# Products over a head's 40 entries: whole stationary blocks of 128 columns, against halves of 64 that alternate between the four quarters of the array

## The chip, the cores and the metric

One core of one Trainium2 chip runs the whole program. The metric is device time in microseconds (us) of one execution of the program, from its first to its last work on the core; the time before is the median of two runs.

## The reference

The program computes two blocks one after the other, all in 32-bit floats. The first is a recurrence over 768 steps for 4 batch entries and 8 heads of 40 entries each; the second sends each of the 3072 result rows (8 heads x 40 = 320 wide) to one of 16 experts, each two matrix products with a relu between.

```python
for t in range(S):                       # S = 768, state is [B, H, D, D], D = 40
    y[:, :, t] = einsum('bhd,bhde->bhe', r_t, state)
    Sa = einsum('bhde,bhe->bhd', state, a_t)
    state = state * w_t[:, :, None, :] - einsum('bhd,bhe->bhde', Sa, b_t)
    state = state + einsum('bhd,bhe->bhde', v_t, k_t)
x = y.transpose(0, 2, 1, 3).reshape(B * S, H * D)
# gate: group by argmax of x @ w_group, expert in it by argmax of x @ w_expert[g]
ye = np.maximum(x @ w1[g, e], 0.0) @ w2[g, e]
out[token] = (weight of group) * (weight of expert) * ye
```

## The kernel before

**Part one** does the recurrence in chunks of 128 steps. There are 6 chunks for each of the 4 batch entries, 24 in all, and one loop (over `u`) goes through them, batch entry by batch entry within a chunk's place. In a chunk, all steps of a head are handled by matrix products of 128 x 128 blocks, one block per head.

A head's 40 entries lie on partitions, and two heads share a tile: the even head of a pair on partitions 0 to 39, the odd one on 64 to 103 (`blk(h)`; `HW` is 64, `NP` the 4 pairs). A chunk does, in the order of the text:

- four **products** over the 40 entries: `GT` from `Kt, At` (named in_k, in_a in the profile), `E` from `At, Bt` (in_a, in_b), `MT` from `Vt, Rt` (in_v, in_r), and near the chunk's end `NT` from `UT, Rt`. Each gives eight 128 x 128 blocks, one per head. `g` is 0 for the even and 1 for the odd heads; each `g` has its own PSUM tile `big` of 4 blocks, and VectorE copies it out through a mask that keeps one triangle (L228);
- VectorE sums the rows of `E` (L239) and makes a factor of them, GpSimd scales `E` by it (L244), TensorE transposes it (L247), ScalarE copies that out as `ET`;
- transposes of in_b, in_k and the running products pq (L217);
- the right-hand side `U` (L260 with the state `ST`, L263 with `GT`), and then seven levels (`lv`) that square `E` and `ET` (L273, L282) and apply `ET` to `U` (L293);
- `U` transposed (L304, `UT`), the next state (L314, L315), the product `NT`, the state transposed (L346), the chunk's result (L328, L332, L334), its transposes (L120) and the gate's logits (L131).

The Tile framework puts each engine's instructions in an order of its own choosing and sets the waits: the next chunk's first product stands around the gate's logits of the chunk before. Two pools of PSUM tiles set when a buffer comes free: five of `big` (512 columns each) and three of `small`. A 32-bit matmul stands in the profile as two loads of the stationary operand (PEld) and two passes of the moving one (PE); the transposes are one load and one pass.

**Part two** sorts the rows by expert and runs the experts by tiles of 128 rows (L558, L566). The change doesn't touch it.

Of the kernel before, what the change touches and what calls it, by code (L numbers as in the profile page):

```python
# [9 lines left out]
F32 = mybir.dt.float32  # L10
I32 = mybir.dt.int32
AX = mybir.AxisListType
ALU = mybir.AluOpType
# [4 lines left out]
# The chunked form of the recurrence divides by running products of w and inverts I + T by  # L18
# powers of T. Both are accurate while w stays within these bounds (128 factors make 1e-15 to
# 1e15) and no row of |T| sums to more than T_MAX. If an input breaks them anywhere, the  # L20
# recurrence is computed again a step at a time, in the reference's order.
# [4 lines left out]
def kernel(  # L26
# [15 lines left out]
    nc = tc.nc  # L42
# [29 lines left out]
    def big(shape):  # L72
        return psum.tile(shape, F32, tag="big", name="big", bufs=5)
# [9 lines left out]
    # up[s, t] = 1 for s < t; low[t, s] = 1 for s < t  # L83
# [10 lines left out]
    # A row of x_all is a token: its vector, its gate weight and its number.  # L94
# [10 lines left out]
    # Rows sorted by expert, each expert's share filled up to whole tiles. Rows that no token  # L105
    # takes keep a zero vector and a number beyond the last token.
# [9 lines left out]
    def transpose_x(pool, src):  # L116
        """[128 tokens, DM] -> [128, NK, 128 tokens]."""
        pt = big([P, NK, P])
        for ko, (k0, kn) in enumerate(KO):
            nc.tensor.transpose(pt[:kn, ko, :], src[:, k0:k0 + kn], ident)  # L120
        t = pool.tile([P, NK, P], F32, tag="xT", name="xT", bufs=2)
        nc.vector.tensor_copy(out=t[:, :NK - 1, :], in_=pt[:, :NK - 1, :])  # L122
        kn = KO[-1][1]
        nc.scalar.copy(out=t[:kn, NK - 1, :], in_=pt[:kn, NK - 1, :])  # L124
        return t
# [10 lines left out]
    # With P_t the product of w over the chunk's steps before t and Q_t that product through t,  # L136
    # A = a P, K = k / Q, B = b / Q and S the state at the chunk's start:
    #   (I + T) U = A S' + G V,         T[t, s] = B_s . A_t,  G[t, s] = K_s . A_t   (s < t)
    #   Y = P (R S + M K - N B),        M[t, s] = r_t . v_s,  N[t, s] = r_t . u_s   (s < t)
    #   next S = (S + V' K - U' B) Q_last  # L140
    # and (I + T)^-1 = (I - T)(I + T^2)(I + T^4)... exactly, T being strictly triangular.
    with ExitStack() as part:
# [18 lines left out]
        # The states of a pair of heads stand as the two diagonal blocks of a square that is zero  # L161
        # elsewhere: ST with the second axis of a state on the partitions, SN with the first.
# [14 lines left out]
        for u in range(NN):  # L177
# [4 lines left out]
            if u < NB:  # L182
                # the partitions that no head's rows take
                for nm in "wakbvr":
                    for q0 in (32, 96):
                        nc.any.memset(d[nm][q0:q0 + 32], 1.0 if nm == "w" else 0.0)
                nc.any.memset(d["pq"][:, :, 0:1], 1.0)
# [10 lines left out]
            # the running products of w (within its bounds), and a, k, b scaled by them  # L198
# [23 lines left out]
            def product(lhs, rhs, g, mask, name, bufs):  # L222
                ps = big([P, NP, P])
                for q in range(NP):
                    nc.tensor.matmul(ps[:, q, :], lhsT=lhs[blk(g), q, :], rhs=rhs[blk(g), q, :],  # L225
                                     start=True, stop=True)
                t = sb.tile([P, NP, P], F32, name=name, bufs=bufs)
                nc.vector.tensor_tensor(t, ps, mask, op=ALU.mult)  # L228
                return t

            # group 0 has the even heads, group 1 the odd ones
            GR = range(2)
            GT = [product(Kt, At, g, up4, "GT", 4) for g in GR]
            # T and its transpose; a row beyond its bound is scaled down to it
            E = [product(At, Bt, g, low4, "E", 6) for g in GR]
# [15 lines left out]
            MT = [product(Vt, Rt, g, up4, "MT", 4) for g in GR]  # L251
# [4 lines left out]
            # the right-hand side, then a factor of the inverse at a time  # L256
# [52 lines left out]
            # the next state  # L309
# [13 lines left out]
            # what the chunk returns  # L323
            NTm = [product(UT, Rt, g, up4, "NT", 4) for g in GR]
# [27 lines left out]
        # how often the bounds are broken  # L352
# [16 lines left out]
    with ExitStack() as part:  # L369
# [5 lines left out]
        # partition (q, b, h) holds rows q DQ .. (q + 1) DQ of the state of (b, h)  # L375
# [59 lines left out]
    with ExitStack() as part:  # L435
# [12 lines left out]
        def choose(vals, name):  # L448
            """The first largest of each token's values as a one-hot, and its softmax weight."""
# [34 lines left out]
        # each token's rank within its expert, then its row in xs  # L484
# [33 lines left out]
        # each tile's expert  # L518
# [81 lines left out]
```

## Time and profile before

| | |
|---|---|
| median of the runs | 2349.13 us (2348.99 to 2349.27) |
| the profiled execution, first to last instruction (span) | 2344.1 us |
| TensorE (PE) busy | 2137.4 us, 91% |
| stationary loads (PEld) busy | 1943.0 us, 83% |
| VectorE busy | 636.2 us, 27% |
| ScalarE busy | 416.2 us, 18% |
| GpSimd busy | 188.8 us, 8% |
| mean granted clock of TensorE | 0.806 of full |

The profiled execution's own time is its span, 2344.1 us; the median of the runs is 5.0 us more, which lies around the span. "Busy" of TensorE counts time in which any pass is under way, and passes overlap. The granted clock is 1.0 or 0.5 of full speed in a stretch (2.4 or 1.2 GHz); values between are means over stretches of both.

### The profile page before, as it was taken

The page shows a single profiled execution, that of the slowest core. Times are in us where ns is not written, and L with a number is a line of the kernel's source. Part 1 is how long each engine was busy: PE and PEld are TensorE (multiplying, and loading weights), DVE is VectorE, ACT ScalarE, POOL GpSimd, SP SyncE. Part 2 cuts the span into 40 slices and gives each one's busy share as a digit, 9 for nine tenths or more (in the row PEclk, how much of TensorE's full clock was granted, in tenths as well). Part 3 has the DMA queues.
Part 4 walks back from the last instruction along what each step waited for, and adds up shares of the span by engine and source line. Part 5 has one row for each costly group of instructions (what it writes and reads, how often), then busy time and mean ns, then how long its engine had stood idle before and what let it go on. Part 6 is the DMA issues. An engine that isn't in the chain of part 4 may idle for free. (4 is left out here: it accounts for less than half of the span.)

```text
span 2344.1 us, 32451 instructions
## 1 busy us (share of the span) xinstructions
PE 2137.4 (91%) x13731; PEld 1943.0 (83%) x13731; DVE 636.2 (27%) x1156; ACT 416.2 (18%) x766; POOL 188.8 (8%) x190
## 2 busy tenths in 40 slices
PE   4999999999999999999999999999505999999998
PEld 3999999999999999999999999999404677777676
DVE  6423333332333333233333232222300111111111
ACT  2222222121222212122212122222000000000000
POOL 3000000000000000000000000000021000000000
PEclk9878876687877868787767787777656999999999
DMA  6000000000000000000000000000042666666661
GB/s 186 21 12 18 21 17 19 20 18 12 18 18 18 21 21 18 12 18 18 18 21 18 12 13 18 4 1 1 29 155 88 212 212 215 200 202 217 205 212 51
DMA packets 143699, 152.68 MB, mean 65 GB/s; under 512 B 33529, under 2 KB 129534, under 8 KB 143552
## 3 DMA queue, kind: packets, MB, share of 16 engines
q1 hardware_dynamic: 133824, 136.21, 18.9%
q10 hardware_dynamic: 6704, 6.46, 1.0%
q0 software_dynamic: 3024, 7.90, 0.9%
q8 instruction: 111, 1.82, 0.3%
q14 instruction: 36, 0.29, 0.0%
HBM read 136.22 MB, written 16.78 MB: 65 GB/s over the span
## 5 line engine op out<-in xcount | busy, mean ns | idle before, releaser
L558 PE MATMUL big<-xT,w1s 128*128 128x128 f32 x1872 | 338.9, 312 | 25.3 <-DVE xT L122 24.6
L558 PEld LDWEIGHTS big<-xT,w1s 128*128 128x128 f32 x1872 | 259.3, 191 | 108.0 <-DVE xT L122 34.7
L293 PE MATMUL small<-U,ET 128*128 128x40 f32 x2688 | 345.9, 290 | 0.6 <-ACT ET L276 0.4
L293 PEld LDWEIGHTS small<-U,ET 128*128 128x128 f32 x2688 | 340.8, 205 | 2.3 <-ACT ET L276 0.5
L273 PE MATMUL big<-ET,E 128*128 128x128 f32 x2304 | 336.6, 292 | 0.0
L273 PEld LDWEIGHTS big<-ET,E 128*128 128x128 f32 x2304 | 300.7, 204 | 0.0
L282 PE MATMUL big<-E,ET 128*128 128x128 f32 x1920 | 266.0, 284 | 0.0
L276 ACT COPY ET<-big 128x512 f32<-128x512 f32 x288 | 168.8, 586 | 481.2 <-PE big L273 481.2
L282 PEld LDWEIGHTS big<-E,ET 128*128 128x128 f32 x1920 | 247.3, 201 | 0.0
L299 DVE TENSOR_TENSOR U<-U,small 128x320 f32<-128x320 f32 x168 | 80.7, 480 | 457.4 <-PE small L293 457.4
L566 PE MATMUL small<-w2s,hT 128*128 128x320 f32 x624 | 180.5, 443 | 0.0
L566 PEld LDWEIGHTS small<-w2s,hT 128*128 128x128 f32 x624 | 116.6, 192 | 48.9 <-issue 1.6
L244 POOL TENSOR_TENSOR E<-E,fit 128x512 f32<-128x512 f32 x48 | 48.9, 1039 | 1199.5 <-DVE fit L242 1188.8
L561 DVE TENSOR_SCALAR hT<-big 128x512 f32<-128x512 f32 x39 | 27.0, 692 | 342.6 <-PE big L558 342.6
L124 ACT COPY xT<-big 64x128 f32<-64x128 f32 x63 | 16.3, 259 | 565.2 <-DVE xT L122 565.2
L120 PE MATMUL big<-ident,xt 128*128 128x128 f32 (+1 forms) x117 | 19.6, 277 | 96.4 <-DMA xt<-xs 96.4
L225 PE MATMUL big<-in_a,in_k 40*128 40x128 f32 x384 | 89.0, 447 | 18.1 <-DMA in_r<-in_rT_dram 18.1
L120 PEld LDWEIGHTS big<-ident,xt 128*128 128x128 f32 (+1 forms) x117 | 14.2, 133 | 105.4 <-DMA xt<-xs 97.5
L334 PE MATMUL small<-nB,NT 128*128 128x40 f32 x384 | 98.6, 351 | 0.0
L225 PEld LDWEIGHTS big<-in_a,in_k 40*128 40x128 f32 x384 | 75.1, 322 | 27.8 <-POOL in_k L212 18.1
L332 PE MATMUL small<-Kn,MT 128*128 128x40 f32 x384 | 94.4, 339 | 0.0
L263 PE MATMUL small<-vn,GT 128*128 128x40 f32 x384 | 94.1, 402 | 0.0
(166 smaller groups left out, 2302.5 us busy)
## 6 DMA issues: line engine op xcount, KB each, us to landing
w2s<-in_w_dram SPq DMA_DIRECT2D x39, 1280.0 KB
w1s<-in_w_dram SPq DMA_DIRECT2D x39, 1024.0 KB
w1s<-in_w_dram SPq DMA_DIRECT2D x39, 256.0 KB
xs<-blank ACTq DMA_DIRECT2D x1, 6279.0 KB
xt<-xs SPq DMA_DIRECT2D x39, 161.0 KB
vn<-in_v_dram SPq DMA_DIRECT2D x24, 160.0 KB
in_w<-in_wT_dram SPq DMA_DIRECT2D x48, 80.0 KB
in_a<-in_aT_dram SPq DMA_DIRECT2D x48, 80.0 KB
```

Of the source, the lines that this page charges most:

```text
L225: nc.tensor.matmul(ps[:, q, :], lhsT=lhs[blk(g), q, :], rhs=rhs[blk(g), q, :], start=True, stop=True)
L244: nc.gpsimd.tensor_tensor(E[g], E[g], fit.broadcast_to([P, NP, P]), op=ALU.mult)
L263: nc.tensor.matmul(ps[:, 2 * i + j, :], lhsT=GT[j][:, i, :], rhs=vn[:, 2 * i + j, :], start=(c == 0), stop=(c == 0 or j == 1))
L273: nc.tensor.matmul(ps[:, q, :], lhsT=E[g][:, q, :], rhs=ET[g][:, q, :], start=True, stop=True)
L276: nc.scalar.copy(out=t, in_=ps)
L282: nc.tensor.matmul(ps[:, q, :], lhsT=ET[g][:, q, :], rhs=E[g][:, q, :], start=True, stop=True)
L293: nc.tensor.matmul(ps[:, h, :], lhsT=ET[h % 2][:, h // 2, :], rhs=U[:, h, :], start=True, stop=True)
L299: nc.vector.tensor_tensor(nx, U, ps, op=ALU.add if lv else ALU.subtract)
L332: nc.tensor.matmul(o, lhsT=MT[j][:, i, :], rhs=Kn[:, i, blk(j)], start=(c == 0), stop=False)
L334: nc.tensor.matmul(o, lhsT=NTm[j][:, i, :], rhs=nB[:, i, blk(j)], start=False, stop=(c == 0 or j == 1))
L558: nc.tensor.matmul(ps[:, f, :], lhsT=w1s[:kn, ko, (f0 + f) * P:(f0 + f + 1) * P], rhs=xT[:kn, ko, :], start=(ko == 0), stop=(ko == NK - 1))
L566: nc.tensor.matmul(ps, lhsT=hT[:, f, :], rhs=w2s[:, f, :], start=(f == 0), stop=(f == FQ - 1))
```

## The change

`product` now makes both groups at once. It takes two PSUM tiles, goes through the pairs `q`, and for each pair issues four matmuls: columns 0 to 63 and then 64 to 127 of the stationary block, and within these the even and then the odd head. A matmul of the change thus has 40 rows and 64 stationary columns (out to 64 PSUM partitions) where one of before had 40 rows and 128 columns; the moving operand keeps its 128 columns. As built, the four matmuls of a pair have tiles of 64 x 64 of the array at rows 0 or 64 and columns 0 or 64; before, a matmul had a tile of 64 x 128 at row 0 or 64. The masks' copies follow when both groups are done. Comments are taken out, which moves line numbers by 9 after the function (L225 becomes L230, L228 becomes L236, L334 becomes L343).

```diff
-            def product(lhs, rhs, g, mask, name, bufs):
-                ps = big([P, NP, P])
+            def product(lhs, rhs, mask, name, bufs):
+                pss = [big([P, NP, P]) for _ in range(2)]
                 for q in range(NP):
-                    nc.tensor.matmul(ps[:, q, :], lhsT=lhs[blk(g), q, :], rhs=rhs[blk(g), q, :],
-                                     start=True, stop=True)
-                t = sb.tile([P, NP, P], F32, name=name, bufs=bufs)
-                nc.vector.tensor_tensor(t, ps, mask, op=ALU.mult)
-                return t
+                    for c0 in (0, HW):
+                        for g in range(2):
+                            nc.tensor.matmul(pss[g][c0:c0 + HW, q, :],
+                                             lhsT=lhs[blk(g), q, c0:c0 + HW],
+                                             rhs=rhs[blk(g), q, :], start=True, stop=True)
+                out = []
+                for g in range(2):
+                    t = sb.tile([P, NP, P], F32, name=name, bufs=bufs)
+                    nc.vector.tensor_tensor(t, pss[g], mask, op=ALU.mult)
+                    out.append(t)
+                return out
...
-            GT = [product(Kt, At, g, up4, "GT", 4) for g in GR]
-            E = [product(At, Bt, g, low4, "E", 6) for g in GR]
+            GT = product(Kt, At, up4, "GT", 4)
+            E = product(At, Bt, low4, "E", 6)
...
-            MT = [product(Vt, Rt, g, up4, "MT", 4) for g in GR]
+            MT = product(Vt, Rt, up4, "MT", 4)
...
-            NTm = [product(UT, Rt, g, up4, "NT", 4) for g in GR]
+            NTm = product(UT, Rt, up4, "NT", 4)
```

On TensorE at the border of two chunks the rows before are these (x_all's transposes and the logits belong to the chunk that ends, in_a, in_k and in_b to the one that begins):

```order
L120 MATMUL big<-ident,x_all 64x128
L225 MATMUL big<-in_a_105,in_k_106 128x128 x3
L131 MATMUL small<-wg,xT 128x20 x2
L225 MATMUL big<-in_a_105,in_k_106 128x128
L131 MATMUL small<-wg,xT 128x20
L225 MATMUL big<-in_a_105,in_k_106 128x128 x4
L225 MATMUL big<-in_b_107,in_a_105 128x128 x8
L260 MATMUL small<-ST_133,in_a_105 128x80
```

and with the change these:

```order
L120 MATMUL big<-ident,x_all 64x128
L230 MATMUL big<-in_a_105,in_k_106 64x128 x5
L131 MATMUL small<-wg,xT 128x20 x2
L230 MATMUL big<-in_a_105,in_k_106 64x128
L131 MATMUL small<-wg,xT 128x20
L230 MATMUL big<-in_a_105,in_k_106 64x128 x10
L230 MATMUL big<-in_b_107,in_a_105 64x128 x16
L269 MATMUL small<-ST_133,in_a_105 128x80
```

The logits still stand in two places inside the first product, now after its fifth and its sixth matmul of 16. On TensorE near the chunk's end, before:

```order
L315 MATMUL small<-U_122,nB 128x80
L225 MATMUL big<-in_r_109,UT 128x128 x8
L346 MATMUL big<-ident,ST_133 128x128
L334 MATMUL small<-nB,NT 128x40
L332 MATMUL small<-Kn,MT 128x40
L346 MATMUL big<-ident,ST_133 128x128 x3
L334 MATMUL small<-nB,NT 128x40
```

and with the change:

```order
L324 MATMUL small<-U_122,nB 128x80
L230 MATMUL big<-in_r_109,UT 64x128 x16
L355 MATMUL big<-ident,ST_133 128x128 x4
L343 MATMUL small<-nB,NT 128x40
L341 MATMUL small<-Kn,MT 128x40
L343 MATMUL small<-nB,NT 128x40
```

All four transposes of the state now stand between the product and the first reader of `NT`. On VectorE the stretch from the copies of `GT` to the copies of `MT` was

```order
L228 TENSOR_TENSOR GT<-big,up 128x512 x2
L228 TENSOR_TENSOR E<-big,low 128x512
L239 TENSOR_REDUCE t_sum<-E 128x4
L228 TENSOR_TENSOR E<-big,low 128x512
L242 TENSOR_SCALAR fit<-t_sum 128x4
L239 TENSOR_REDUCE t_sum<-E 128x4
L243 RECIPROCAL fit<-fit 128x4
L242 TENSOR_SCALAR fit<-t_sum 128x4
```

and is

```order
L236 TENSOR_TENSOR GT<-big,up 128x512 x2
L236 TENSOR_TENSOR E<-big,low 128x512 x2
L248 TENSOR_REDUCE t_sum<-E 128x4 x2
L251 TENSOR_SCALAR fit<-t_sum 128x4 x2
L252 RECIPROCAL fit<-fit 128x4 x2
```

Both copies of `E` now stand ahead of the first row sum. ScalarE and GpSimd keep their orders.

## Rows read from the trace of the kernel before

**Rows 1.** The page's busy line of engines, and two lines of its 40 slices.

```profile
PE 2137.4 (91%) x13731; PEld 1943.0 (83%) x13731; DVE 636.2 (27%) x1156; ACT 416.2 (18%) x766; POOL 188.8 (8%) x190
...
PE   4999999999999999999999999999505999999998
...
PEclk9878876687877868787767787777656999999999
```

**Rows 2.** Groups of instructions by form, whole span: busy us, mean ns of one.

```profile
L225 PE MATMUL big<-in_a,in_k 40*128 40x128 f32 x384 | 89.0, 447 | 18.1 <-DMA in_r<-in_rT_dram 18.1
...
L225 PE MATMUL big<-in_b,in_a 40*128 40x128 f32 x384 | 74.2, 437 | 0.0
...
L225 PE MATMUL big<-in_r,UT 40*128 40x128 f32 x384 | 60.4, 374 | 2.7 <-ACT UT L307 2.7
...
L244 POOL TENSOR_TENSOR E<-E,fit 128x512 f32<-128x512 f32 x48 | 48.9, 1039 | 1199.5 <-DVE fit L242 1188.8 <-DVE fit L243 10.7
...
L228 DVE TENSOR_TENSOR NT<-big,up 128x512 f32<-128x512 f32 x48 | 33.0, 690 | 29.1 <-PE big L225 28.4
```

**Rows 3.** Timeline of TensorE, start of a chunk: start us, length us, passes.

```profile
639.05 1.65 PE L225 MATMUL big<-in_a,in_k 40*128 40x128 f32 x6
640.62 1.04 PE L131 MATMUL small<-wg,xT 128*128 128x20 f32 x4
641.60 0.81 PE L225 MATMUL big<-in_a,in_k 40*128 40x128 f32 x4
...
642.84 0.42 PE L225 MATMUL big<-in_a,in_k 40*128 40x128 f32 x1
643.00 0.42 PE L225 MATMUL big<-in_b,in_a 40*128 40x128 f32 x1
643.05 0.42 PE L225 MATMUL big<-in_a,in_k 40*128 40x128 f32 x1
643.22 0.42 PE L225 MATMUL big<-in_b,in_a 40*128 40x128 f32 x1
...
645.65 0.71 PE L260 MATMUL small<-ST,in_a 128*128 128x80 f32 x2
...
650.79 1.95 PE L247 MATMUL big<-ident,E 128*128 128x128 f32 x8
652.67 3.09 PE L225 MATMUL big<-in_r,in_v 40*128 40x128 f32 x16
655.69 1.12 PE L217 MATMUL big<-ident,in_b 128*128 128x128 f32 x4
...
658.27 0.98 PE L293 MATMUL small<-U,ET 128*128 128x40 f32 x8
```

**Rows 4.** Busy time in stretches of two chunks; PEclk is the granted clock.

```profile
571.10:583.60 12.50, 12.50 (x65) 11.62 (x66) 4.89 (x11) 0.44 (x2) 2.04 (x2) 0.50 0.00 0
583.60:590.90 7.30, 7.30 (x37) 6.75 (x37) 1.49 (x3) 2.52 (x5) 0.00 (x0) 0.50 0.18 50
590.90:600.20 9.30, 9.30 (x46) 9.30 (x45) 6.58 (x7) 2.23 (x5) 2.95 (x2) 0.50 0.14 42
...
650.80:658.10 7.30, 7.30 (x37) 6.74 (x38) 1.57 (x3) 2.60 (x5) 0.00 (x0) 0.50 0.18 53
658.20:667.50 9.30, 9.30 (x85) 9.30 (x84) 6.97 (x9) 3.63 (x7) 2.94 (x2) 1.00 0.14 41
```

**Rows 5.** Timeline of TensorE, the product `NT` in the chunk before.

```profile
631.20 1.71 PE L225 MATMUL big<-in_r,UT 40*128 40x128 f32 x16
632.84 0.33 PE L346 MATMUL big<-ident,ST 128*128 128x128 f32 x1
633.14 0.42 PE L334 MATMUL small<-nB,NT 128*128 128x40 f32 x2
```

**Rows 6.** Passes that read `UT`: ns least/median/most, first and last start.

```profile
L225 PE MATMUL big<-in_r,UT x384: 272/417/579, 88.3 to 1657.9; 40*128 40x128 f32 x192
```

**Rows 7.** Who waited for whom, TensorE: us in total, times, longest.

```profile
PE big L247 <- POOL E L244: 15.4, 2, 10.6
```

## The prediction

> **What bounds the kernel now.** First the page: TensorE is busy for 91% of the span, and its line of slices is 9 from the second slice to the thirtieth, which is the recurrence, while no other engine passes 27% [rows 1]. So time comes off only where TensorE's own work gets shorter, or where its clock is higher. The line of the granted clock is 6 to 9 there: a mixture of full and half clock. Stretches of one and the next chunk show what the mixture is [rows 4]: in the chunk from 571.1 the clock is at half until 600.2; in the next one it is back at full from 658.2, at work that the first still did at half (590.9 to 600.2: 46 passes in 9.3 us; 658.2 to 667.5: 85 in the same time). The chunk's first stretch, with three of its four products, is at half in both (12.5 us from 571.1, and the 7.3 us before 658.1).
>
> Then the products. Each of the four groups counts 384 passes [rows 2], 24 chunks of 16: eight matmuls of two passes. In the timeline [rows 3], one pass after the other takes 0.214 us at half clock (L260 and L263: 24 passes from 645.65 to 650.79), and 0.109 at full (9.3 us over 85 passes [rows 4]). The product `MT`, 652.67 to 655.69, takes 3.02 us, less than 16 x 0.214 = 3.42. The reason stands a little higher up: in_a,in_k has passes at 642.84 and 643.05, in_b,in_a at 643.00 and 643.22, each 0.21 apart, so two run side by side. They are the odd heads of one product and the even ones of the next, in different row halves of the array. The kernel before thus has some of what the change is after, wherever one group's queue still holds passes as the other's begin.
>
> **The change, part by part.** *Passes.* Each product goes from 16 passes to 32. A pass still streams 128 moving columns, so I keep 0.214 us for it, and what decides is how many go side by side: with four, 32 passes need 8 turns, as many as the old 16 would need in pairs of row halves. No row shows two passes in the column halves of one row half. The nearest rows are those of two row halves, which do run together [rows 3]; from these the bounds are four at a time and two at a time. I take between three and four in the forecast, and two for the first rival.
>
> *Switches.* Going from the product to the gate's logits and back costs more than the passes: six passes from 639.05 to 640.62 take 1.57 us where 6 x 0.214 is 1.28, so 0.29 at half clock [rows 3], which I take as 0.15 at full.
>
> *`MT`*, at half clock: 8 x 0.214 + 0.29 = 2.00 us with four at a time against 3.02: 1.02 saved. With three at a time, 10.7 turns, 2.57: 0.45 saved.
>
> *`NT`*: at full clock 631.20 to 632.84, 1.64 us [rows 5]; at half like `MT`. The median of its passes, 417 ns, is that of the half clock [rows 6, 3], so about half of the chunks have it there. At full, 8 x 0.11 + 0.15 = 1.03 saves 0.61, and three at a time save 0.32; the mean with the half clock is 0.81 and 0.38.
>
> *`GT`, `E` and the logits in between*: 639.05 to 645.65, 6.60 us [rows 3]. New: ten passes ahead of the logits, four of them in one quarter, 4 x 0.214 + 0.29 = 1.15; the logits as now, 640.62 to 641.60, 0.98; then 54 passes in 14 turns and a switch, 3.29. That is 5.42, 1.18 saved. But the logits' last matmul (64 rows, all columns) now stands between two of 64 columns, which before had its own kind of tile on both sides. If each change of tile costs a switch, one product matmul and the logits' one stand alone (two turns and a switch each, 0.72 twice) and the rest is 13 turns and a switch, 3.07: 1.15 + 0.98 + 1.44 + 3.07 = 6.64, nothing saved. The middle is 0.57. With three at a time it is 4 turns more, 0.86: a loss of 0.29.
> The Trainium skill says that a change of tiling mode, not just of the tile, drains the array (TensorEngine Tiling (Array Packing), Key Properties). The 0.29 us agree for whole array against row halves; none of these rows has a column half. By that rule alone the stage saves nothing, 14 us less in the sum than the middle.
>
> *Sum of the passes*: 0.57 + 1.02 + 0.81 = 2.40 us a chunk, 58 us over 24 chunks, with four at a time; -0.29 + 0.45 + 0.38 = 0.54, 13 us, with three. I take the middle, 35.
>
> *Copies.* The even heads' copy no longer starts while the odd ones' product runs. For `NT`, two copies of 0.69 us [rows 2] begin together after the product, and the four transposes that now all stand ahead of the first reader cover 4 x 0.214 = 0.86 at half clock, enough, but 0.45 at full: the first reader waits some 0.3 us and the next, for the second copy, as much. 0.6 us in half of the chunks is 7 us. For `GT` the copies are hidden by the product `E`, which takes longer than 1.4 us. For `E`, two copies and two row sums of about the same size, 2.8 us, and one scaling of 1.04 [rows 2] are 3.8 before L247 can start; TensorE has 5.14 us of L260 and L263 meanwhile, and today waits for that scaling only twice in the whole span [rows 7]. Nothing, as long as the clock is at half there. At the very start, VectorE now puts the second chunk's reciprocal ahead of the first copies; that is once in 24 chunks, and left out.
>
> *Clock.* `L247`, `MT` and `L217` stand one behind the other from 650.79 to 658.27, and in that chunk the clock rose just as they ended; in the chunk of 571.1 the same work ended near 591 and the clock rose only at 600.2 [rows 3, 4]. With `MT` shortened by up to a third and more of the array at work in it, I expect the earlier rise more often. Its worth: 46 passes at 0.109 are 5.0 us instead of 9.3, 4.3 for a chunk of the first kind; if half of the chunks are, 52 us in all. I take two thirds, 35; nothing to 52 is the range.
>
> Together 35 - 7 + 35 = 63 us. The profiled execution would go from 2344.1 to 2281 us, and with the 5 us that lie around the span the forecast is **2286 us**. Its own range: 58 + 52 gives 2239; 13 - 7 and no clock gives 2343.
>
> **Rivals.** *The column halves take turns* (slower). Two passes at a time, one per row half: `MT` 16 x 0.214 + 0.29 = 3.71, 0.69 lost; `NT` 0.48 lost in the mean (1.91 at full); `GT` and `E` 1.57 + 0.98 + 27 x 0.214 + 0.29 = 8.62, 2.0 lost, and 2.6 with half of the extra switches (0.6); the middle is 2.3. That is 3.5 a chunk, 84 us, and 7 for the copies: **2440 us**. It decides as soon as fewer than about 2.6 of the passes run at once, since 32 passes then take more than the 3.02 us of today. For it: nothing in the trace shows column halves together, and twice as many instructions have to be issued. Against it: issue has slack, as the side-by-side stretches show [rows 3].
> The Trainium skill says that a stationary load overlaps matmuls under way only when the row groups differ (TensorE: Matmul & The Clock Gate, Part 3, "What overlaps and what doesn't"). That would bring about this rival. The trace doesn't bear it out for whole blocks, where loads and passes are both busy for all of 9.30 us [rows 4]; no row has column halves. The same part has measured speedups of packed rows and columns far above two, which speaks for the forecast.
>
> *The clock is up before `E` ends* (much faster). With more of the array at work at once, the clock may rise already in the first product stage, and then 645.65 to 658.1, 12.4 us at half clock, takes half of that: 6.2 a chunk, 149 us, beside the 52 and the 28 of above. L260 and L263 would then cover only 24 x 0.11 = 2.6 us of the 3.8 and more that `E` needs to come back, a wait of 1.2 to 2.4, some 43 us. **2163 us**. For it: in every chunk this stage is the one whose work becomes densest. Against: the logits break it up, and in neither chunk did the clock rise there [rows 4].
>
> *The switches eat it*: quarters run together, but the first stage gains nothing, the rise stays where it is, and the copies take back the rest: 2330 to 2349 us, within 2%.
>
> **How the numbers follow.** Forecast 0.40, column halves take turns 0.25, early clock 0.22, eaten 0.13. Two per cent, what a measurement of this kernel tells from no change, is 47 us: below 2302 lie three quarters of the forecast (0.30) and the early clock, 0.52 together; within it a quarter of the forecast and the last case, 0.23; above 2396 the first rival, 0.25. Cases of both signs hold most of the chance, so the range has to take in both rivals' values: 2150 to 2445; below lies an early clock without the wait for `E`, above it passes that go one at a time. The likeliest case's own range is 2239 to 2343.
>
> **What would show it.** In the timeline of after, `MT` in 2.0 to 2.6 us at half clock and starts of four passes within one 0.21: right. 3.7 us and pairs: the first rival. The granted clock of the stretch from L256 to L217, and where it rises in two neighbouring chunks, show the clock's term; a rise ahead of L269 is the second rival, with waits of L256 for GpSimd. The first stage, from the product's first pass to L269, 5.4 us or 6.6, tells whether the logits' last matmul costs switches. The prediction is wrong if the products' own time goes up, or if it falls by 2 us a chunk and the clock gives it back by falling earlier near the chunk's end.

## The result and the profile after

The changed kernel takes 2233.53 us (median of 2225.5 and 2241.55) against 2349.13: a ratio of 0.951, 95% interval 0.948 to 0.955. That is 116 us, where 63 were forecast. The profiled execution took 2225.5 us, with a span of 2223.5 and a mean granted clock of 0.845 (before 0.806).

The page of after, first the engines' busy time, then the slices of TensorE's clock, then two groups:

```profile
PE 2008.3 (90%) x15267; PEld 1792.5 (81%) x15267; DVE 604.5 (27%) x1156; ACT 414.1 (19%) x766; POOL 184.9 (8%) x190
...
PEclk9888887788888878878888787777558999999999
...
L230 PE MATMUL big<-in_a,in_k 40*64 40x128 f32 x768 | 78.5, 429 | 18.1 <-POOL in_k L212 18.1
...
L343 PE MATMUL small<-nB,NT 128*128 128x40 f32 x384 | 90.4, 326 | 4.4 <-DVE NT L236 3.2
```

Against [rows 1] TensorE stays the bound, with 129 us less of busy time, and its clock reads 8 more often where it read 7 and 6. The passes have doubled, 768 a group for 384 [rows 2], and each still lasts 417 ns at half clock, as the passes of `MT` below show. `L343`, which reads `NT`, waits 3.2 us in all for VectorE's copies.

The products by form over the whole span (busy us, mean ns of one); they answer to [rows 2]:

```profile
L230 PE MATMUL big<-in_b,in_a 40*64 40x128 f32 x768 | 55.6, 417 | 0.0
L230 PE MATMUL big<-in_r,in_v 40*64 40x128 f32 x768 | 46.7, 419 | 0.0
L230 PE MATMUL big<-in_r,UT 40*64 40x128 f32 x768 | 31.8, 313 | 2.7 <-ACT UT L316 2.7
```

`E` fell from 74.2 to 55.6, `NT` from 60.4 to 31.8, `GT` from 89.0 to 78.5 only; `MT`, which before also had 74.2 in this view, to 46.7.

The timeline of TensorE at a chunk's start (start us, length us, passes), at half clock up to the last row as [rows 3] are:

```profile
595.93 1.11 PE L230 MATMUL big<-in_a,in_k 40*64 40x128 f32 x10
596.98 1.04 PE L131 MATMUL small<-wg,xT 128*128 128x20 f32 x4
597.95 0.69 PE L230 MATMUL big<-in_a,in_k 40*64 40x128 f32 x2
598.56 0.61 PE L131 MATMUL small<-wg,xT 64*128 64x20 f32 x2
599.10 1.33 PE L230 MATMUL big<-in_a,in_k 40*64 40x128 f32 x18
...
602.28 0.71 PE L269 MATMUL small<-ST,in_a 128*128 128x80 f32 x2
...
609.30 1.99 PE L230 MATMUL big<-in_r,in_v 40*64 40x128 f32 x32
611.22 1.11 PE L217 MATMUL big<-ident,in_b 128*128 128x128 f32 x4
```

`MT` takes 609.30 to 611.22, 1.92 us for 3.02. The product stage up to `L269` takes 6.35 us for 6.60, and the third to the fifth row show why it is so little: two lone passes and the logits' last matmul, four passes in all, fill 597.95 to 599.10, 1.15 us.

The same passes of `MT`, asked for by line (ns least/median/most, first and last start us):

```profile
L230 PE MATMUL big<-in_r,in_v x32: 417/417/472, 609.3 to 610.9; 40*64 40x128 f32 x32
```

32 starts in 1.6 us: in the single records four begin within 20 ns, and after the first turn four follow on four every 213 ns. The four quarters do work together.

`NT` in the chunk before, at full clock, up to the transposes of the state:

```profile
588.31 1.10 PE L230 MATMUL big<-in_r,UT 40*64 40x128 f32 x32
589.58 0.63 PE L355 MATMUL big<-ident,ST 128*128 128x128 f32 x4 [0.17 <-PE big L230]
```

That is 1.27 us, where [rows 5] had 1.64.

Last the clock. Stretches of after, cut where the granted clock changes (columns as in [rows 4]; the clock is the third number from the end); chunks start at 595.9, 661.5 and 723.8:

```profile
551.10:595.40 44.30, 42.89 (x405) 41.89 (x398) 17.01 (x28) 13.29 (x23) 2.76 (x2) 1.00 0.08 21
595.40:622.70 27.30, 27.30 (x191) 25.17 (x191) 11.56 (x20) 5.03 (x11) 3.44 (x3) 0.50 0.10 28
622.70:660.30 37.60, 36.60 (x344) 35.73 (x342) 9.78 (x19) 10.50 (x18) 1.36 (x2) 1.00 0.05 10
660.30:680.80 20.50, 20.08 (x157) 17.96 (x157) 7.62 (x18) 3.82 (x8) 2.04 (x2) 0.50 0.12 34
680.80:721.70 40.90, 40.07 (x376) 39.32 (x376) 13.95 (x21) 11.51 (x20) 2.75 (x2) 1.00 0.05 13
721.70:738.80 17.10, 16.52 (x141) 14.53 (x140) 5.10 (x12) 2.22 (x6) 2.03 (x2) 0.50 0.07 20
```

The same cut of before; its chunks start at 571.9, 639.0 and 708.4:

```profile
555.80:600.20 44.40, 43.81 (x217) 41.87 (x216) 15.88 (x26) 6.35 (x13) 4.98 (x4) 0.50 0.10 25
600.20:637.80 37.60, 36.85 (x327) 36.23 (x326) 9.78 (x19) 10.37 (x18) 0.00 (x0) 1.00 0.04 8
637.80:658.20 20.40, 19.98 (x101) 18.55 (x102) 6.92 (x15) 3.13 (x7) 2.04 (x2) 0.50 0.10 28
658.20:692.40 34.20, 33.62 (x301) 33.48 (x300) 13.76 (x20) 11.25 (x20) 2.94 (x2) 1.00 0.05 14
```

Both kernels repeat a pattern through most of the recurrence, and each spends 65 us of it at half clock: before over two chunks (44.4 and 20.4), after over three (27.3, 20.5 and 17.1). Before, the clock falls 16 us ahead of the end of every second chunk, at 555.8 and 692.4, so that `NT` and the outputs run at half there. After, within its pattern, it falls 0.5 to 2.1 us ahead of a chunk's end each time. Part two of the kernel is the same in both (before from 1801, 543 us; after from 1681, 542).

The 22 chunks from the start of the second to that of the twenty-fourth give the account. One row of before, then one of after:

```profile
95.23:1600.51 1505.28, 1477.43 (x10211) 1429.99 (x10210) 485.45 (x824) 340.25 (x613) 103.64 (x84) 0.75 0.06 16
```

```profile
93.43:1483.00 1389.57, 1353.84 (x11620) 1286.49 (x11619) 455.89 (x824) 338.22 (x613) 99.74 (x84) 0.81 0.07 17
```

They differ by 115.7 us, nearly all of the 120.6 by which the two profiled spans differ. TensorE's idle time in them grew from 27.9 to 35.7.

### The profile page after: what moved, and what is told of

Same layout as the page of the kernel before. It is cut to its first block, busy times and chain, and to the rows that moved or that the text cites. A ratio compares the mean times of both kernels' runs of the same rounds, so it can differ in the third digit from the quotient of the medians.

```text
span 2223.5 us, 35519 instructions
## 1 busy us (share of the span) xinstructions
PE 2008.3 (90%) x15267; PEld 1792.5 (81%) x15267; DVE 604.5 (27%) x1156; ACT 414.1 (19%) x766; POOL 184.9 (8%) x190
## 5 line engine op out<-in xcount | busy, mean ns | idle before, releaser
L302 PE MATMUL small<-U,ET 128*128 128x40 f32 x2688 | 335.2, 284 | 0.6 <-ACT ET L285 0.4
L302 PEld LDWEIGHTS small<-U,ET 128*128 128x128 f32 x2688 | 329.6, 199 | 2.3 <-ACT ET L285 0.5
L282 PE MATMUL big<-ET,E 128*128 128x128 f32 x2304 | 323.8, 287 | 0.0
L282 PEld LDWEIGHTS big<-ET,E 128*128 128x128 f32 x2304 | 289.9, 199 | 0.0
L291 PE MATMUL big<-E,ET 128*128 128x128 f32 x1920 | 260.5, 280 | 0.0
L291 PEld LDWEIGHTS big<-E,ET 128*128 128x128 f32 x1920 | 241.1, 197 | 0.0
L297 DVE COPY E<-big 128x512 f32<-128x512 f32 x96 | 66.4, 691 | 118.1 <-PE big L291 116.7
L230 PE MATMUL big<-in_a,in_k 40*64 40x128 f32 x768 | 78.5, 429 | 18.1 <-POOL in_k L212 18.1
L272 PEld LDWEIGHTS small<-vn,GT 128*128 128x128 f32 x384 | 91.9, 332 | 3.5 <-DVE GT L236 3.4
L343 PE MATMUL small<-nB,NT 128*128 128x40 f32 x384 | 90.4, 326 | 4.4 <-DVE NT L236 3.2
```

The lines of the kernel that those rows point to most:

```text
L230: nc.tensor.matmul(pss[g][c0:c0 + HW, q, :], lhsT=lhs[blk(g), q, c0:c0 + HW], rhs=rhs[blk(g), q, :], start=True, stop=True)
L272: nc.tensor.matmul(ps[:, 2 * i + j, :], lhsT=GT[j][:, i, :], rhs=vn[:, 2 * i + j, :], start=(c == 0), stop=(c == 0 or j == 1))
L282: nc.tensor.matmul(ps[:, q, :], lhsT=E[g][:, q, :], rhs=ET[g][:, q, :], start=True, stop=True)
L291: nc.tensor.matmul(ps[:, q, :], lhsT=ET[g][:, q, :], rhs=E[g][:, q, :], start=True, stop=True)
L297: nc.vector.tensor_copy(out=t, in_=ps)
L302: nc.tensor.matmul(ps[:, h, :], lhsT=ET[h % 2][:, h // 2, :], rhs=U[:, h, :], start=True, stop=True)
```

## The experiments

The theory: four quarters run at once, which is worth some 2 us a chunk by itself, and the larger half of the gain is the clock, which the shorter and fuller stages move. The rivals: (a) it is the order, one row half and the other in turn, that gains, and the split of the columns is worth nothing; (b) column halves overlap only because the row halves alternate, and take turns within one; (c) the gain is the passes alone, and the clock follows them without a weight of its own. All times below are medians; the kernel before had 2354.76, 2350.31 and 2356.43 us in the three groups of runs, each run beside its own.

### What the quarters do

**Row halves alone.** Whole blocks of 128 columns, even and odd heads in turn.

```diff
                 for q in range(NP):
-                    for c0 in (0, HW):
-                        for g in range(2):
-                            nc.tensor.matmul(pss[g][c0:c0 + HW, q, :],
-                                             lhsT=lhs[blk(g), q, c0:c0 + HW],
-                                             rhs=rhs[blk(g), q, :], start=True, stop=True)
+                    for g in range(2):
+                        nc.tensor.matmul(pss[g][:, q, :], lhsT=lhs[blk(g), q, :],
+                                         rhs=rhs[blk(g), q, :], start=True, stop=True)
```

> The products alternate between the two row halves only; the stationary block keeps its 128 columns, so there are 16 passes a product, not 32. If what pays is that both row halves are fed at once, 16 passes need 8 turns like the change's 32: MT takes 1.9 to 2.0 us at half clock, and the time is that of the change within 15 us (2220 to 2250). If the column halves themselves are needed (because the queue feeds two whole row halves no better than before), MT stays between 2.3 and 3.0 us and the time lies at 2280 to 2349.

2264.62 us, 0.963 (0.959 to 0.967) of before: some three quarters of the change's gain without its column halves (0.037 of 0.049). The timeline of this kernel, at half clock:

```profile
666.30 1.22 PE L229 MATMUL big<-in_a,in_k 40*128 40x128 f32 x6
...
668.42 0.58 PE L229 MATMUL big<-in_a,in_k 40*128 40x128 f32 x1
668.43 0.61 PE L131 MATMUL small<-wg,xT 64*128 64x20 f32 x2
...
671.71 0.71 PE L267 MATMUL small<-ST,in_a 128*128 128x80 f32 x2
...
678.73 2.08 PE L229 MATMUL big<-in_r,in_v 40*128 40x128 f32 x16
680.74 1.12 PE L217 MATMUL big<-ident,in_b 128*128 128x128 f32 x4
```

`MT` takes 2.01 us, 0.09 more than in quarters, and the first stage 5.41, 0.94 less: the logits' last matmul (64 rows, all columns) begins 0.01 us after a product's pass and runs beside it. So its passes are cheaper than those of the change, and still the kernel is slower than the change, 0.963 against 0.951, 28 us, and outside the 2220 to 2250 us that were expected with such an `MT`. Its stretches at half clock say where that is:

```profile
664.20:691.50 27.30, 26.71 (x144) 25.14 (x144) 13.06 (x21) 5.19 (x11) 4.98 (x4) 0.50 0.11 31
...
729.10:756.40 27.30, 26.71 (x143) 25.14 (x143) 13.07 (x21) 4.99 (x10) 4.99 (x4) 0.50 0.11 31
```

Here the clock rises in the squarings in each chunk, 27.3 us at half each time, while after has 27.3, 20.5 and 17.1; read stretch by stretch, the 22 chunks named above have 614 us at half clock against 526. Rival (a) is right of the passes and wrong of the time.

**Column halves alone.** The loop over the groups goes outermost, so that only the column halves of one row half alternate.

```diff
-                for q in range(NP):
-                    for c0 in (0, HW):
-                        for g in range(2):
+                for g in range(2):
+                    for q in range(NP):
+                        for c0 in (0, HW):
```

> Columns in halves as in the change, but one group's eight matmuls first and then the other's, so neighbours in the queue share a row half and differ in the column half. If column halves of one row half run together, each group needs 8 turns and MT takes 2.9 to 3.7 us at half clock: a time like before, 2330 to 2400. If they take turns, each group needs 16 turns, MT takes 5 to 7 us, and the time is over 2500.

2365.2 us, 1.005 (1.003 to 1.007). The timeline of `MT` and `NT` in this kernel at half clock, and `MT`'s passes by line:

```profile
717.08 2.89 PE L230 MATMUL big<-in_r,in_v 40*64 40x128 f32 x32
719.91 1.11 PE L217 MATMUL big<-ident,in_b 128*128 128x128 f32 x4
...
762.74 2.89 PE L230 MATMUL big<-in_r,UT 40*64 40x128 f32 x32
765.57 0.65 PE L343 MATMUL small<-nB,NT 128*128 128x40 f32 x2
```

```profile
L230 PE MATMUL big<-in_r,in_v x32: 417/418/473, 717.1 to 719.6; 40*64 40x128 f32 x32
```

32 passes start within 2.5 us; one at a time they would need 32 x 0.213 = 6.8. In the single records two begin 7 ns apart, every 0.207 to 0.213 us: two column halves of one row half do run together. `MT` and `NT` (2.83 us each) also overlap their two groups as before did, with 3.02. The slower kernel comes from the first stage, 702.72 to 710.07, which takes 7.35 us for 6.60, 0.75 in nearly every chunk, with the clock nearly as in before (750 us at half in the 22 chunks, before 741). Rival (b) falls: what the first rival of the prediction feared does not happen in this order either.

**One product in quarters.** `MT` as in the change, the other three as before.

```diff
+            def product_old(lhs, rhs, g, mask, name, bufs):
...
-            GT = product(Kt, At, up4, "GT", 4)
+            GT = [product_old(Kt, At, g, up4, "GT", 4) for g in GR]
-            E = product(At, Bt, low4, "E", 6)
+            E = [product_old(At, Bt, g, low4, "E", 6) for g in GR]
...
-            NTm = product(UT, Rt, up4, "NT", 4)
+            NTm = [product_old(UT, Rt, g, up4, "NT", 4) for g in GR]
```

> Only the product MT is made in quarters; GT, E and NT are as before. MT saves 1.1 us a chunk at half clock, 26 us by itself. If the clock's share comes from MT standing between the whole-block transposes L247 and L217, the clock now rises with L217 in most chunks and the time is 2260 to 2300. If the clock's share needs the other products too, the time is 2315 to 2330.

2307.51 us, 0.982 (0.976 to 0.987), 47 us less than before. `MT` takes 1.92 us, which is 24 x 1.10 = 26 us; the other 21 go with the clock (0.77 for 0.75 in the 22 chunks). The clock thus moves with one product, in a measure between the cases. It moves both ways: the first halves of the 22 chunks stand at half clock for 417 us, before for 530, but the second halves for 269, before for 211. With `MT` alone the earlier rise is partly paid back by an earlier fall, which the prediction had among its signs of being wrong; in after it isn't.

**The change once more**, unaltered, beside the runs of the next part.

> The changed kernel once more, beside the others of this call. If its gain is the clock's, with rises and falls in the same places, the time is 2233 within 10 us and the half-clock time is 23 to 25 us a chunk.

2242.75 us, 0.952 (0.947 to 0.957). Its profiled execution came into the pattern of three chunks only at 514.8, that of the first run at 363.3; over the 22 chunks it took 1405.32 us at a clock of 0.80 against 1389.57 at 0.81. Its chunks stand at half clock for 559 us (25.4 a chunk, a little over what was expected) against 526; half of the difference is 16 us, which is all that the 22 chunks differ by. The spread of the same kernel, some 8 us either way, is where the clock's changes fall.

### What the clock does

If the clock has a weight of its own, it must move at unchanged passes. The products read 40 of each 64 rows, and the matmuls with 40 columns a head leave 24 of 64 unused; both can be filled with zeros.

**Before, with 64 rows.**

```diff
+        def blk64(h):
+            return slice((h % 2) * HW, (h % 2) * HW + HW)
...
-                    nc.tensor.matmul(ps[:, q, :], lhsT=lhs[blk(g), q, :], rhs=rhs[blk(g), q, :],
+                    nc.tensor.matmul(ps[:, q, :], lhsT=lhs[blk64(g), q, :], rhs=rhs[blk64(g), q, :],
```

> The kernel before with one edit: its products run over 64 rows of a row half instead of 40, the other 24 rows hold zeros. Passes, turns and order stay. If the clock's rise depends on how much of the array the products put to work, the clock rises earlier in some chunks and the time falls by 10 to 60 us with each pass as long as before at either clock. If only the length of the products counts, the time is 2349 within 5 us.

2318.85 us, 0.983 (0.978 to 0.988). The stages are those of before: the first stage 6.60 (690.64 to 697.25), `NT` 3.02 and 1.64, and `MT` at half clock 3.02:

```profile
704.26 3.09 PE L228 MATMUL big<-in_r,in_v 64*128 64x128 f32 x16
707.28 1.11 PE L220 MATMUL big<-ident,in_b 128*128 128x128 f32 x4
```

Only the clock moved, 0.77 for 0.75 in the 22 chunks: they stand at half clock for 671 us, before for 741, which is worth 35, and they take 32 less. Rival (c) falls.

**After, with 64 rows:** the same edit in the changed kernel's `product`.

```diff
-                                             lhsT=lhs[blk(g), q, c0:c0 + HW],
-                                             rhs=rhs[blk(g), q, :], start=True, stop=True)
+                                             lhsT=lhs[blk64(g), q, c0:c0 + HW],
+                                             rhs=rhs[blk64(g), q, :], start=True, stop=True)
```

> The changed kernel with its products over 64 rows of a row half, 24 of them zeros: no pass, turn or order changes, and a pass takes no longer. If what pays is how much of the array works when L256, MT and L230's first stage run, the clock rises earlier again: 2080 to 2200 us with MT still at 1.92 us at half clock. If the clock only follows how tightly passes stand in time, the time is that of the change, 2220 to 2245.

2181.89 us, 0.928 (0.924 to 0.932) of before; `MT` is still 1.92 us at half clock. Of the 526 us at half clock in after's 22 chunks 398 are left, and all that went did so from the first halves of the chunks (290 for 428).

**After, with 64 columns a head** in the right-hand side, the next state and the result; `V_pad` is `vn` with zeros behind each head's 40.

```diff
-            ps = small([P, H, D])
+            ps = small([P, H, HW])
...
-                                     rhs=ST[b_][:, i, :, :D], start=True, stop=False)
+                                     rhs=ST[b_][:, i, :, :], start=True, stop=False)
...
-                    nc.tensor.matmul(o, lhsT=NTm[j][:, i, :], rhs=nB[:, i, blk(j)],
+                    nc.tensor.matmul(o, lhsT=NTm[j][:, i, :], rhs=nB[:, i, j * HW:(j + 1) * HW],
```

> The changed kernel, but the passes of the chunk's result (L337, L341, L343), of the right-hand side (L269, L272) and of the next state stream 64 columns a head instead of 40, the rest zeros. These passes take 0.112 us at full and 0.213 at half clock now, as long as whole-block passes of 128 columns, so their time shouldn't change. If the clock falls at the chunk's end because these passes leave the array idle, it now stays at full there: NT and what follows run at full in nearly all chunks, and the time is 2080 to 2190. If the fall has another cause, 2230 to 2250.

2132.17 us, 0.908 (0.904 to 0.911). The 22 chunks stand at half clock for 273 us where after had 526: 52 for 98 in the second halves of the chunks, and 222 for 428 in the first. In seven of them the whole first stage runs at full clock.

**Both in the changed kernel.**

```diff
+                                             lhsT=lhs[blk64(g), q, c0:c0 + HW],
...
+            ps = small([P, H, HW])
```

> Both edits of the two other kernels of this call. If the clock is what the recurrence pays for, it now stays at full for nearly all of a chunk, and 22 chunks come near their length at full clock, 51 to 54 us each instead of 63: 1960 to 2060 us. If the clock falls in the first product stage anyway, 2080 to 2180. If neither edit moves the clock, 2230 to 2250.

2075.19 us, 0.882 (0.879 to 0.885), at a mean clock of 0.943. The timeline, now at full clock:

```profile
497.23 0.65 PE L238 MATMUL big<-in_a,in_k 64*64 64x128 f32 x10
...
500.73 0.49 PE L277 MATMUL small<-ST,in_a 128*128 128x128 f32 x2
...
505.18 0.66 PE L264 MATMUL big<-ident,E 128*128 128x128 f32 x4 [1.43 <-POOL E L261]
506.18 0.66 PE L264 MATMUL big<-ident,E 128*128 128x128 f32 x4 [0.34 <-POOL E L261]
506.76 1.10 PE L238 MATMUL big<-in_r,in_v 64*64 64x128 f32 x32
```

The pairs of passes in the result take 0.39 us at full clock with 64 columns a head, as they do in after with 40: the added columns are free. And the prediction's second rival is here as it was priced: `L264`, the transposes of `E`, waits 1.43 and 0.34 us for GpSimd's scaling, 24 x 1.77 = 42 us, where the rival had 43. The time lies between two of the expected ranges: 99 us of the 22 chunks are still at half clock, worth 50, and the wait is some 40 (39.5 in the 22 chunks); without the two a chunk would take 52.7 us, within the 51 to 54 of the expectation.

### With the clock held

If the clock is full throughout, the passes alone should decide between the orders.

**Row halves, both paddings:** the first experiment's loop with `blk64`, and the wide columns.

```diff
+                    for g in range(2):
+                        nc.tensor.matmul(pss[g][:, q, :], lhsT=lhs[blk64(g), q, :],
+                                         rhs=rhs[blk64(g), q, :], start=True, stop=True)
...
+            ps = small([P, H, HW])
```

> The kernel with 64 columns a head and 64 rows, but its products in the two row halves with whole blocks of 128 columns. If column halves are worth no turn of their own, and the 20 to 30 us between quarters and row halves were a matter of when the clock rose, then with the clock held at full the row halves are as fast or faster (the logits' last matmul then keeps the products' kind of tile): 2045 to 2075 us. If the column halves are worth time in themselves, it is 2085 to 2110.

2047.34 us, 0.869 (0.866 to 0.871) of before: less than the quarters with the same paddings, 0.882, and by the medians 28 us. The order of the two has turned round. The timeline of its first stage and of `MT`, and its longest stretch at full clock:

```profile
537.90 0.71 PE L237 MATMUL big<-in_a,in_k 64*128 64x128 f32 x6
...
540.85 0.49 PE L275 MATMUL small<-ST,in_a 128*128 128x128 f32 x2
...
546.87 1.16 PE L237 MATMUL big<-in_r,in_v 64*128 64x128 f32 x16
547.96 0.66 PE L225 MATMUL big<-ident,in_b 128*128 128x128 f32 x4
```

```profile
220.50:1200.10 979.60, 922.41 (x8385) 885.73 (x8384) 398.62 (x690) 273.63 (x500) 89.05 (x72) 1.00 0.08 22
```

2.95 us for the stage, against 3.50 in quarters (497.23 to 500.73 above), and 1.09 for `MT`, against 1.04 (506.76 to 507.80). The column halves save 0.05 us a product, and the stage with the logits costs them 0.55. That is 22 x 0.50 = 11 us of the 34 between the two in the 22 chunks. The clock wasn't held quite alike: row halves stand at half for 48 us there, quarters for 99, and half of the difference, 25 us, is the larger share. So the passes favour the row halves, and with both paddings the clock does too; why it does, when without paddings it favoured the quarters, no run shows.

**Row halves where the logits are, quarters elsewhere**, without padding.

```diff
+            def product(lhs, rhs, mask, name, bufs, width):
...
+                    for c0 in range(0, P, width):
...
+            GT = product(Kt, At, up4, "GT", 4, P)
+            E = product(At, Bt, low4, "E", 6, P)
+            MT = product(Vt, Rt, up4, "MT", 4, HW)
+            NTm = product(UT, Rt, up4, "NT", 4, HW)
```

> The changed kernel with GT and E in row halves of 128 columns, MT and NT in quarters. The first stage should fall from 6.35 to 5.41 us at half clock, 0.94 a chunk, 23 us in all, if the logits' last matmul was what cost it switches. If only the work counted, 2210 to 2225; if the places where the clock rises go back to those of the row halves everywhere, 2240 to 2270, with less work and more half-clock time.

2260.2 us, 0.960 (0.954 to 0.966). It joins the cheaper stage (5.41 us) to the cheaper `MT` (1.92) and is no faster than row halves alone. A stretch at half clock:

```profile
733.30:760.60 27.30, 26.72 (x160) 25.03 (x160) 12.05 (x21) 4.99 (x10) 3.28 (x3) 0.50 0.10 31
```

The clock rises in the squarings again, after 27.3 us. So, without padding, quarters in the first stage, where they cost 0.94 us a chunk, are what goes with the earlier rise. That the loss lies in where the clock rises is shown; what in the stage moves it is not.

**The mixture with both paddings.**

```diff
+                            nc.tensor.matmul(pss[g][c0:c0 + width, q, :],
+                                             lhsT=lhs[blk64(g), q, c0:c0 + width],
+                                             rhs=rhs[blk64(g), q, :], start=True, stop=True)
...
+            ps = small([P, H, HW])
```

> The same mixture with 64 columns a head and 64 rows, the clock held at full. GT and E take 0.4 to 0.5 us less than the 3.50 of the quarters at full clock, but E then comes back no earlier from GpSimd, so that L256's wait may grow by what is saved: 2055 to 2080 us.

2039.44 us, 0.866 (0.863 to 0.868), the fastest, and 16 us under the expected range: the wait for the scaling did not grow, and only 27 us of the 22 chunks are at half clock, against 99 in quarters. One stretch of it, nine chunks at full clock without a break:

```profile
217.00:705.10 488.10, 459.78 (x4481) 440.68 (x4473) 193.63 (x351) 136.67 (x250) 42.19 (x36) 1.00 0.09 22
```

and its largest wait on another engine in the 22 chunks (us, times, longest; 39.5 with quarters):

```profile
PE big L264 <- POOL E L261: 39.2, 39, 2.1
```

**`E` ahead of `GT`** in that kernel, so that `GT`'s sixteen passes stand between `E` and its transposes.

```diff
-            GT = product(Kt, At, up4, "GT", 4, P)
             E = product(At, Bt, low4, "E", 6, P)
+            GT = product(Kt, At, up4, "GT", 4, P)
```

> The same, with the product E ahead of GT, so that its copies, row sums and scaling start about 1 us earlier. At full clock L256 waited 1.8 us a chunk for the scaling: with 1 us less of it 24 us less, 2030 to 2055. If the copies of GT come in between on VectorE, nothing is gained: 2055 to 2080.

2077.13 us, 0.882 (0.879 to 0.884): 38 us slower. The wait moved to the reader of `GT`, and a little is left at the transposes of `E` (22 chunks again):

```profile
PE small L279 <- DVE GT L244: 28.9, 43, 1.7
...
PE big L263 <- POOL E L260: 3.8, 12, 0.3
```

That is 32.7 us for 39.2, only 6.5 less of waiting, while over the 22 chunks the clock is 0.95 for 0.99: they stand at half for 119 us where the mixture has 27, which costs 46. The two together make 39 us, and the 22 chunks take 38 more.

The 22 chunks of the runs side by side (from the same view as the two rows above):

| kernel | 22 chunks, us | granted clock |
|---|---|---|
| before | 1505.28 | 0.75 |
| column halves alone | 1518.04 | 0.75 |
| before, 64 rows | 1473.51 | 0.77 |
| `MT` alone in quarters | 1463.92 | 0.77 |
| row halves, then quarters | 1425.38 | 0.78 |
| row halves | 1419.21 | 0.78 |
| after | 1389.57 | 0.81 |
| after, 64 rows | 1343.42 | 0.85 |
| after, 64 columns a head | 1292.65 | 0.89 |
| after, both | 1249.11 | 0.96 |
| mixture, both, `E` first | 1242.47 | 0.95 |
| row halves, both | 1214.85 | 0.98 |
| mixture, both | 1204.87 | 0.99 |

## Why the prediction was right, and where it was too small

The time fell, as forecast, and 2233.53 us lies within the whole range of 2150 to 2445. That range is wide, since it takes in both rivals; of the likeliest case's own, 2239 to 2343, the time is 6 us below the lower end. The passes came out near the case of four at a time; some 50 us of what the clock gave had no term in the sum, and that it went the same way was luck.

**Four at a time** was right. `MT` took 1.92 us where 2.00 stood for four and 2.57 for three; the sum took the middle of the two, so it gave away part of a step that held. `NT` at full clock took 1.27 (588.31 to 589.58) where 1.03 was forecast, and 1.92 at half.

The Trainium skill's rule that a stationary load overlaps matmuls under way only when the row groups differ (TensorE: Matmul & The Clock Gate, Part 3, "What overlaps and what doesn't") stood behind the first rival. The measurement decides against it for column halves: two of one row half start 7 ns apart.

**The switches** were sized as half: 0.57 us saved in the first stage, between 1.18 and nothing. Measured are 0.25 (6.35 us). The upper bound, 6.64, is nearly the truth: the two lone passes and the two of the logits' matmul take 1.15 us, which is 4 x 0.214 and one switch of 0.29, where the bound had a second switch. The kernels with row halves there, 5.41 us, come within 0.01 of the other bound. Key Properties of TensorEngine Tiling (Array Packing) in the Trainium skill, by which a change of mode drains the array, agrees with 597.95 to 599.10.

**The sum of the passes**, 2.40 us a chunk with four at a time, came to 1.10 + 0.25 + 0.73 = 2.08 (`NT`: the mean of 1.10 at half and 0.37 at full). That is 46 us in the 22 chunks and 50 in all, where 35 were taken.

**The copies**: 7 us lost were forecast. TensorE's idle time in the 22 chunks grew by 8. Of it 2.4 us are `L343`'s wait for the copies (3.2 in the whole span), and 2.6 are short waits of the state's transposes for the product ahead of them (0.17 at 589.58), which had no term.

**The clock** is the term that was mis-sized: 35 us taken, 52 at most. Read stretch by stretch, the 22 chunks of before have 741 us at half clock, 530 in the first halves of the chunks and 211 in the second; after has 428 and 98. In the first halves 102 us went, of which 22 x (1.10 + 0.25) = 30 are the shorter passes themselves; the other 72 are work that now runs at full clock, worth half of that, 36 us. This is the earlier rise, and it came as forecast. In the second halves 113 us went, some 12 of them as shorter `NT`; the other 101 are worth 50 us, and these had no term. In before the clock fell at `L304` in every second chunk, ahead of `NT` and the outputs; after, this fall is gone from the pattern. The prediction priced where the clock rises, named an earlier fall as what could undo the gain, and had no price for a later one. `NT` now has full clock in 16 of the 22 chunks, before in 9.

The four sums, 46 + 36 + 50 - 8 = 124, are 8 more than the 116 measured: the split is no better than that, and latencies that don't shrink with the clock would be a reason, which no run tested. Two sizes in the prediction's working are off without bearing on it: with a switch of 0.29 the break-even with 3.02 us lies at 2.5 passes at once, not 2.6, and `NT` had the half clock in 13 of the 22 chunks where half was taken.

**The rivals.** Column halves that take turns: refuted by the second experiment. The clock up before `E` ends: not in after, where it rises in `MT` at the earliest (551.1); but with the paddings it happened, and its wait for GpSimd came at the forecast price, 39.5 us in the 22 chunks. Switches that eat it: in the first stage nearly, in the sum not.

What stays open is why the rise comes in `MT` in one chunk of three in the changed kernel, and in the squarings in each when row halves stand in the first stage; and why with both paddings it is the row halves that keep the clock at full for longer.

## What to carry over

When TensorE's clock changes within a loop, look at both its edges: price the work ahead of the rise and the work behind the fall, and where the loop repeats over several chunks, read the whole pattern. Small matmuls whose passes keep their time when columns or rows are added can be filled with zeros, which brought the clock of the 22 chunks from 0.80 to 0.96 here, more than the reordering did. Alternating between row halves gave nearly all that the array had to give; before going to quarters, look at which matmul of another tile stands among them, since there the quarters cost 0.94 us more than row halves, and they save 0.09 on a product without such a neighbour.

## What the runs showed of the hardware

- Two column halves of one row half run together as two row halves do: pairs 7 ns apart, four quarters within 20 ns, and four after four every 213 ns at half clock. For 40 rows, four quarters are hardly better than two row halves (1.92 and 2.01 us for a product at half clock, 1.04 and 1.09 at full).
- A matmul of 64 rows and all columns ran beside row-half passes (0.01 us apart) but not beside quarters: with two lone passes it took 1.15 us at half clock.
- Rows and columns of zeros alone, at unchanged pass times, took the granted clock of the 22 chunks from 0.80 to 0.96, and the kernel from 2242.75 to 2075.19 us on the same chip.
- Before, TensorE was busy for 91% of the span [rows 1] and its clock fell in every chunk or two; with both paddings it stayed at full for 488 us at a stretch with the products mixed, and for 980 us with row halves alone.
